# Eight per-partition multiplies, or sixteen, become one broadcast product: the second pass of a decode-attention backward kernel

## The chip, the cores and the metric

The kernel runs on one core of a Trainium2 chip. The metric is device time in microseconds (us), the median of several executions; lower is better. "The kernel before" and "the changed kernel" are the two whose difference is studied.

Names in the views: PE is the matrix engine and PEld its loading of weights; VectorE (DVE), ACT and POOL are the other compute engines; SP only issues transfers here. PSUM holds PE's results (`d_ps` and the other `_ps` tiles in the views). "arena" is one large on-chip buffer from which the kernel cuts its tiles. A transfer is issued on an engine's queue; "lands" means its end in the trace. A store is compute-gated when it has to wait for a result.

## The reference

The reference is the forward pass and all gradients of one decode step: pre-norm attention of one token over the last 4096 positions of a 32768-position cache, then a gated bilinear feed-forward block.

```python
W = 4096; Hq, Hkv, Sk, Dh, D, F = 16, 8, 32768, 256, 448, 1792
k = repeat(k_cache[:, :, Sk - W:, :], 2); v = repeat(v_cache[:, :, Sk - W:, :], 2)
p = softmax(q @ k.T * Dh ** -0.5); o = p @ v
h  = x + o.reshape(1, 1, Hq * Dh) @ wo              # q from layernorm(x) @ wq
h2 = h + ((hn @ w_gate) * (hn @ w_up)) @ w_down      # hn = layernorm(h)
_out, _vjp = jax.vjp(_f, A_x, A_k_cache, A_v_cache, A_wq, A_wo, B_w_gate, B_w_up, B_w_down)
return (_out, *_vjp(grad_out))                       # all tensors bf16
```

What matters for the time is the size of two outputs. The gradients of the two caches have the full shape (1, 8, 32768, 256), 134 MB each. Seven eighths of each lie outside the window and are zeros, but must be written all the same.

## The kernel before

Zeros go out on POOL's queue from the start, a block of 2 MB each, and need no compute. A few zero stores are kept for the end of SP's queue:

```python
late_jobs = [(out_2, G - 1, 5, 7, 2 * ZW), (out_3, G - 1, 0, 6, 2 * ZW), (out_3, G - 1, 6, 7, ZW)]
...
def send_fills(n0, n1, halves=False):
    for reg in fills[n0:n1]:
        ...
            ZQ.dma_start(out=reg, in_=zeros)         # ZQ = nc.gpsimd, POOL's queue (L132)

send_fills(0, HALF0)
send_fills(HALF0, HALF1, True)
# ... first pass over the 8 heads, feed-forward block, then: send_fills(HALF1, len(fills))
```

The second pass makes the gradients of K and V in the window, head by head. For each head it builds eight masked right-hand sides, one for each value of `l`, multiplies by them on PE, copies PSUM to the staging buffers on VectorE and ACT, and stores them through SP's queue (`LD`):

```python
RB_ = Rbig[it % 2]
for l in range(8):
    nc.vector.tensor_scalar(out=RB_[:, l, :], in0=R_sb[:], scalar1=tl_f[:, l:l + 1], scalar2=None, op0=ALU.mult)   # L629
stV, stK = V_sb, kv_at(dK_off[it % 2])
for l in range(8):
    for qp in range(2):
        d_ps = ps_d.tile([128, 2, 2, Dh], f32, tag="d")
        for qi in range(2):
            q = 2 * qp + qi
            nc.tensor.matmul(d_ps[:, qi]..., lhsT=rT[32 * q:32 * (q + 1), :], rhs=RB_[32 * q:32 * (q + 1), l, :], ...)   # L636
        ...                                          # copies: ACT L640, L641; VectorE L643, L644
for o_ap, st_ in ((out_3, stV), (out_2, stK)):
    LD.dma_start(out=o_ap[0, g, Sk - W:, :]..., in_=st_)      # L646: 2.1 MB each
for job in plan[it]:
    job()                                            # weight-gradient rows: dwo, dw_down, dwq, ...
...
for o, g, n0, n1, f in late_jobs:                    # L656: the zero stores on SP's queue
    ...
```

The jobs for dwo and dw_down scale one row of 448 elements by 16 or 14 per-partition factors (the helper's line is L532). Their staging buffers are former V buffers, so a job waits until an earlier store has landed (in the kernel before 13.5 us in all ahead of dwo's rows and 7.1 us ahead of dw_down's). A framework schedules the instructions of each engine when the kernel is built.

Of the kernel before, what the change touches and what calls it, by code (L numbers as in the profile page):

```python
# [10 lines left out]
ALU = mybir.AluOpType  # L11
ACT = mybir.ActivationFunctionType

D = 448
# [7 lines left out]
NF = 14  # L22
# [11 lines left out]
def kernel(  # L34
        ctx, tc, A_x, A_k_cache, A_v_cache, A_wq, A_wo, B_x, B_w_gate, B_w_up, B_w_down, grad_out,
           out_0, out_1, out_2, out_3, out_4, out_5, out_6, out_7, out_8):
    nc = tc.nc
# [15 lines left out]
    def ar(off, n):  # L53
        return arena[:, off:off + n]

    def kv_at(off):
        return ar(off, T * Dh).rearrange("p (t d) -> p t d", d=Dh)
# [38 lines left out]
    dh2_bc = const.tile([128, D], bf16)  # L96
# [53 lines left out]
    tl_f = const.tile([128, 8], f32)  # L150
# [88 lines left out]
    def fill_vpad(i, src):  # L239

        nc.vector.tensor_copy(out=vpad[i][:].rearrange("p e (c w) -> p e c w", w=18)[:, :, :, 0:2],
                              in_=src.unsqueeze(2).to_broadcast([128, 2, 8, 2]))

    def dots(X_sb, XT_slots, pad, rows, cols_pool, cols_tag, evac):

        rows_ps = ps_s.tile([16, 512], f32, tag="rows")
        for q in range(8):
            XT = XT_slots[q % 3]
            tr_ps = ps_tr.tile([128, 2, 4, 128], bf16, tag="tr")
            for dh in range(2):  # L250
                for i in range(4):
                    nc.tensor.transpose(tr_ps[:, dh, i, :], X_sb[:, 4 * q + i, dh * 128:(dh + 1) * 128], ident_bf[:])  # L252
            evac(q, XT, tr_ps[:])
            for dh in range(2):
                nc.tensor.matmul(rows_ps[:], lhsT=pad[:, dh, 16 * q:16 * q + 16], rhs=XT[:, dh].rearrange("p t k -> p (t k)"),  # L255
                                 start=(q == 0 and dh == 0), stop=(q == 7 and dh == 1))
        nc.vector.tensor_copy(out=rows, in_=rows_ps[:])  # L257
        cols_ps = cols_pool.tile([128, 4, 8, 2], f32, tag=cols_tag, name="cols_ps")
        for i in range(4):
            nc.tensor.transpose(cols_ps[:, i].rearrange("p c h -> p (c h)"), rows[:, i * 128:(i + 1) * 128], ident_f[0:16, 0:16])  # L260
        return cols_ps
# [94 lines left out]
    with tc.tile_pool(name="ps_mid", bufs=3, space=bass.MemoryType.PSUM) as ps_mid, \  # L356
# [11 lines left out]
        oX_f = const.tile([128, 32], f32)  # L368
# [17 lines left out]
        hh_f = const.tile([128, NF], f32)  # L386
# [4 lines left out]
        for n in range(len(BLOCKS)):  # L391
# [3 lines left out]
            for b in range(nb):  # L395
                nc.vector.tensor_tensor_reduce(out=dgb[:, 0:D], in0=wd[:, b, :], in1=dh2_bc[:], scale=1.0, scalar=0.0,
                                               op0=ALU.mult, op1=ALU.add, accum_out=d_hh[:, b0 + b:b0 + b + 1])
# [11 lines left out]
            for i in range(2):  # L409
                nc.vector.tensor_tensor(out=diag[:, 0:w].rearrange("p (m b) -> p m b", b=nb), in0=ident_f[:].unsqueeze(2).to_broadcast([128, 128, nb]),  # L410
                                        in1=dgu_f[:, i, cs].unsqueeze(1).to_broadcast([128, 128, nb]), op=ALU.mult)
# [6 lines left out]
            for c in range(4):  # L418
# [3 lines left out]
                                               op0=ALU.mult, op1=ALU.add, accum_out=dhn[0:kp, c, n:n + 1])  # L422
# [9 lines left out]
        dh_bc = const.tile([128, D], bf16)  # L432
# [18 lines left out]
        for jc in range(32):  # L451
            nc.vector.tensor_tensor_reduce(out=wo_sb[:, jc, :], in0=wo_sb[:, jc, :], in1=dh_bc[:], scale=1.0, scalar=0.0,  # L452
                                           op0=ALU.mult, op1=ALU.add, accum_out=doX_f[:, jc:jc + 1])
# [3 lines left out]
                                in1=m8_f[:].unsqueeze(2).to_broadcast([128, 8, 32]), op=ALU.mult)  # L457
# [13 lines left out]
        for dh in range(2):  # L471
# [11 lines left out]
                                scalar1=SCALE, scalar2=None, op0=ALU.mult)  # L483
# [4 lines left out]
    with tc.tile_pool(name="work2", bufs=2) as work2, tc.tile_pool(name="lnw", bufs=1) as lnw, \  # L488
# [17 lines left out]
        for c in range(3):  # L506
            nc.vector.tensor_tensor_reduce(out=wq2A[:, c, :], in0=wq2A[:, c, :], in1=dq_bc, scale=1.0, scalar=0.0,  # L507
                                           op0=ALU.mult, op1=ALU.add, accum_out=dn1[:, c:c + 1])
        for h in range(2):
            nc.vector.tensor_tensor_reduce(out=wq2A[:, 0, 0:HJ], in0=wq2B, in1=dq_bc[:, h * HJ:(h + 1) * HJ], scale=1.0, scalar=0.0,  # L510
                                           op0=ALU.mult, op1=ALU.add, accum_out=dn1[:, 3 + h:4 + h])
# [15 lines left out]
        def buffer():  # L527
            wst_ctr[0] += 1
            return wst[(wst_ctr[0] - 1) % 2]

        def scale_into(out, src, col):
            nc.vector.tensor_scalar(out=out, in0=src, scalar1=col, scalar2=None, op0=ALU.mult)  # L532

        def job_o(n):
            def run():
                buf = buffer()
                for j in range(16):
                    scale_into(buf[:, j * D:(j + 1) * D], dh_bc[:], oX_f[:, 16 * n + j:16 * n + j + 1])
                LD.dma_start(out=out_5.rearrange("(p j) n -> p (j n)", j=32)[:, 16 * n * D:16 * (n + 1) * D], in_=buf[:, 0:16 * D])
            return run  # L540

        def job_d():
            buf = buffer()
            for j in range(NF):
                scale_into(buf[:, j * D:(j + 1) * D], dh2_bc[:], hh_f[:, j:j + 1])
            for f0, nb in BLOCKS:
                b0 = f0 // 128
                LD.dma_start(out=out_8[f0:f0 + 128 * nb, :].rearrange("(p b) n -> p (b n)", b=nb), in_=buf[:, b0 * D:(b0 + nb) * D])
# [38 lines left out]
        def job_qB():  # L587
# [4 lines left out]
            LD.dma_start(out=out_4[384:D, :].rearrange("r (h j) -> (r h) j", h=2), in_=buf[:, 2 * HJ:3 * HJ])  # L592

        plan = [[], [], [job_o(0)], [job_o(1)], [job_d, job_q], [expand_dg, job_qB, job_g(0)], [job_g(1)], []]

        order = [2, 3, 4, 5, 6, 7, 0, 1]
        V2_off = [V_off[g] for g in order[:6]] + [MB, MB + 16 * KB]
        for it, g in enumerate(order):
            V_sb = kv_at(V2_off[it])
            fill_vpad(it % 2, doT_bf[:, :, 2 * g:2 * g + 2])  # L600

            def evac(q, XT, ps):
                if q % 2:
                    nc.scalar.copy(out=XT, in_=ps)  # L604
                else:
                    nc.vector.tensor_copy(out=XT, in_=ps)  # L606
            dpT_ps = dots(V_sb, VT_slot, vpad[it % 2], rows2, ps_t, "tmp", evac)

            pds = work2.tile([128, 4, 8, 4], bf16, tag="pds")
            pv = pT_all[:, g].rearrange("p (q l) h -> p q l h", q=4)  # L610
            tmp = work2.tile([128, T, 2], f32, tag="tmp2")
            nc.vector.tensor_tensor(out=tmp[:], in0=dpT_ps[:].rearrange("p q l h -> p (q l) h"),
                                    in1=delta_bc[:, 2 * g:2 * g + 2].unsqueeze(1).to_broadcast([128, T, 2]), op=ALU.subtract)
            nc.vector.tensor_copy(out=pds[:, :, :, 0:2], in_=pv)
            nc.vector.tensor_tensor(out=pds[:, :, :, 2:4], in0=tmp[:].rearrange("p (q l) h -> p q l h", q=4), in1=pv, op=ALU.mult)
            r_ps = ps_t.tile([128, 128], bf16, tag="tmp")
            nc.tensor.transpose(r_ps[:], pds[:].rearrange("p q l i -> p (q l i)"), ident_bf[:])
            rT = work2.tile([128, 128], bf16, tag="rT")
            nc.vector.tensor_copy(out=rT[:], in_=r_ps[:])
            nc.vector.tensor_copy(out=Zr, in_=Z4[:, :, :, g, :].rearrange("p w e i -> p (w e) i").unsqueeze(2).to_broadcast([128, 4, 32, 4]))  # L620
            R_ps = ps_t.tile([128, 2, 2, 128], f32, tag="tmp")
            for w in range(2):
                for dh in range(2):
                    nc.tensor.matmul(R_ps[:, w, dh, :], lhsT=Zr[:, 2 * w + dh].rearrange("p k i -> p (k i)"), rhs=ident_bf[:], start=True, stop=True)
            R_sb = work2.tile([128, 512], bf16, tag="R", bufs=1)
            nc.scalar.copy(out=R_sb[:], in_=R_ps[:].rearrange("p w e n -> p (w e n)"))
            RB_ = Rbig[it % 2]
            for l in range(8):
                nc.vector.tensor_scalar(out=RB_[:, l, :], in0=R_sb[:], scalar1=tl_f[:, l:l + 1], scalar2=None, op0=ALU.mult)  # L629
            stV, stK = V_sb, kv_at(dK_off[it % 2])  # L630
            for l in range(8):
                for qp in range(2):
# [3 lines that stand above are left out]
                        nc.tensor.matmul(d_ps[:, qi].rearrange("p w d -> p (w d)"), lhsT=rT[32 * q:32 * (q + 1), :], rhs=RB_[32 * q:32 * (q + 1), l, :],  # L636
                                         start=True, stop=True)
                    t = 4 * l + 2 * qp
                    if qp:
                        nc.scalar.copy(out=stV[:, t:t + 2, :], in_=d_ps[:, :, 0, :])  # L640
                        nc.scalar.copy(out=stK[:, t:t + 2, :], in_=d_ps[:, :, 1, :])  # L641
                    else:
                        nc.vector.tensor_copy(out=stV[:, t:t + 2, :], in_=d_ps[:, :, 0, :])  # L643
                        nc.vector.tensor_copy(out=stK[:, t:t + 2, :], in_=d_ps[:, :, 1, :])  # L644
            for o_ap, st_ in ((out_3, stV), (out_2, stK)):
                LD.dma_start(out=o_ap[0, g, Sk - W:, :].rearrange("(p t) d -> p t d", t=T), in_=st_)  # L646
            for job in plan[it]:
                job()
            if it == 6:

                nc.vector.memset(ar(ZW, ZW), 0.0)
# [34 lines left out]
```

## Time and profile before

| | kernel before |
|---|---|
| time, median | 800.08 us |
| bytes moved | 334.80 MB, 216.01 MB of them POOL's zero fills |
| transfer engines | busy in all slices, 419 GB/s on average |
| VectorE (DVE) | 408.4 us busy, 51% |

From the profile's page of the kernel before: busy time of each engine, then the transfers in 40 equal slices of the span (tenths of busy share of the 16 transfer engines, then GB/s), then the totals.

```profile
PE 469.3 (59%) x3159; PEld 242.1 (30%) x3182; DVE 408.4 (51%) x728; ACT 196.2 (25%) x309; POOL 61.4 (8%) x112
...
DMA  9999999999999999999999999999999999999996
GB/s 351 429 432 429 430 430 429 429 429 427 429 422 425 426 419 417 413 423 424 422 423 408 430 429 429 432 424 428 423 429 420 426 424 427 419 424 426 427 436 261
DMA packets 29354, 334.80 MB, mean 419 GB/s; under 512 B 2819, under 2 KB 5894, under 8 KB 7814
```

No compute engine is near full, and the digit of the transfers is 9 everywhere but in the last slice. That could still hide gaps of a few us in the part that the change touches. So here is the busy time in 20 us stretches of the second pass of the kernel before. After each engine's busy us and count come the granted clock of PE, the transfer engines' share (it reads up to 1.03 here) and their GB/s.

```profile
core 0: us, PE busy (x) PEld busy (x) DVE busy (x) ACT busy (x) POOL busy (x), PEclk, DMA share, GB/s
480.00:500.00 20.00, 17.50 (x155) 8.51 (x155) 17.46 (x39) 14.33 (x22) 2.13 (x4) 1.00 1.01 428
...
620.00:640.00 20.00, 0.29 (x1) 0.13 (x2) 3.55 (x2) 0.00 (x0) 1.06 (x2) 0.50 1.02 430
...
720.00:740.00 20.00, 2.54 (x16) 0.52 (x16) 5.60 (x9) 4.84 (x10) 0.00 (x0) 0.50 1.03 426
...
760.00:780.00 20.00, 0.00 (x0) 0.00 (x0) 0.00 (x0) 0.00 (x0) 0.00 (x0) 0.50 1.02 436
780.00:798.40 18.40, 0.00 (x0) 0.00 (x0) 0.00 (x0) 0.00 (x0) 0.00 (x0) 0.50 0.57 246
```

From 620 to 640 us compute all but stopped, waiting for stores to land (one of VectorE's waits for a landing, 23.9 us long, ends at 635.8 us), and the transfer engines didn't notice: share 1.02, 430 GB/s. They had fills to send, issued at 622.5 and 631.8 us.

The timelines of POOL and of SP's queue in the kernel before show how long that lasts. Columns: start, duration, engine, line, operation, count.

```profile
688.23 0.54 POOL L132 DMA_DIRECT2D out_dram<-arena  x1 [16.88 <-issue]
...
727.89 6.93 SPq L646 DMA_DIRECT2D out_dram<-arena  x2
736.57 8.42 SPq L656 DMA_DIRECT2D out_dram<-arena  x3
```

The last fill is issued at 688 us, the last two stores that wait for compute at 728 and 731 us, then zeros. From there to 798 us the queue drains. Bytes issued less bytes landed, summed from the trace's issues and packets, came to 13.6 MB at 730 us. The three zero stores behind the last gated store are not in that sum.

The instructions that the change touches, kernel before, by line and shape: count, busy us, mean ns of one, then idle time of the engine before them. L304 is a tensor product of the first pass that multiplies bf16 by a float32 operand broadcast, as the new products do, so it is a price for the new form: 2284 ns for 2048 columns.

```profile
L304 DVE TENSOR_TENSOR arena<-arena,p_f 128x2048 bf16<-128x2048 bf16 x64 | 145.2, 2284 | 58.7 <-PE M_ps L309 58.7
L629 DVE TENSOR_SCALAR arena<-R_sb,tl_f 128x512 bf16<-128x512 bf16 x64 | 17.8, 347 | 2.1 <-ACT R_sb L626 1.9
L532 DVE TENSOR_SCALAR arena<-dh_bc,oX_f 128x448 bf16<-128x448 bf16 x32 | 8.8, 328 | 13.5 <-DMA out_dram<-arena 13.5
L532 DVE TENSOR_SCALAR arena<-dh_bc,hh_f 128x448 bf16<-128x448 bf16 x14 | 3.9, 329 | 7.1 <-DMA out_dram<-arena 7.1
```

Eight of the L629 multiplies overlap in time: one takes 347 ns, so eight would take 2.78 us end to end, and they fill 2.19. From the timeline of VectorE (columns as in the timelines above), the eight of the first head:

```profile
477.36 2.19 DVE L629 TENSOR_SCALAR arena<-R_sb,tl_f 128x512 bf16<-128x512 bf16 x8 [0.33 <-ACT R_sb L626]
```

### The profile page before, as it was taken

What the parts mean: (1) busy time and instruction counts of PE and PEld (TensorE: products, weight loads), DVE (VectorE), ACT (ScalarE), POOL (GpSimd) and SP (SyncE); (2) the same over time, 40 slices, a digit from 0 to 9 for tenths busy, and PEclk for the clock granted to TensorE, in tenths of its full rate; (3) what the DMA queues carried; (4) which work ended last, traced back from release to release, by engine and by line L of the source; (5) the groups of instructions that cost most, each with busy time, mean ns of one, the idle gap of its engine ahead of it and who ended that gap; (6) DMA issues with size and microseconds to landing.
All of it is one profiled execution on the core that took longest, in us unless ns stands there. A gap on an engine that the chain in (4) does not pass through costs nothing.

```text
span 798.4 us, 7905 instructions
## 1 busy us (share of the span) xinstructions
PE 469.3 (59%) x3159; PEld 242.1 (30%) x3182; DVE 408.4 (51%) x728; ACT 196.2 (25%) x309; POOL 61.4 (8%) x112
## 2 busy tenths in 40 slices
PE   0459999999999998532319568565236027261000
PEld 0334545545445444311207434332103012020000
DVE  2116584765846783143791579467574139573000
ACT  0142314124132201000101127463333016242000
POOL 4000000010101111100210001000000000000000
PEclk9989999999999999555557869785558558565555
DMA  9999999999999999999999999999999999999996
GB/s 351 429 432 429 430 430 429 429 429 427 429 422 425 426 419 417 413 423 424 422 423 408 430 429 429 432 424 428 423 429 420 426 424 427 419 424 426 427 436 261
DMA packets 29354, 334.80 MB, mean 419 GB/s; under 512 B 2819, under 2 KB 5894, under 8 KB 7814
## 3 DMA queue, kind: packets, MB, share of 16 engines
q0 software_dynamic: 16496, 216.01, 64.0%
q1 hardware_dynamic: 11382, 116.68, 34.8%
q10 hardware_dynamic: 1440, 1.61, 0.6%
q8 instruction: 25, 0.41, 0.2%
q14 instruction: 11, 0.09, 0.0%
HBM read 53.69 MB, written 280.59 MB: 419 GB/s over the span
## 4 chain that ended last, share of the span: by engine, by line
PE 40%; DMA 28%; DVE 15%; ACT 4%; issue 2%; another core or an unknown queue 0%; SPq 0%; ACTq 0%; DVEq 0%
DMA out_dram<-arena 18%; PE M_ps L309 13%; PE ok_ps L313 8%; PE rows_ps L255 7%; PE tr_ps L252 5%; DMA dh_bc<-in_grad_out_dram 4%; ACT arena L269 3%; DVE arena L643 2%; DVE arena L644 2%; DMA arena<-in_A_wo_dram 2%; DVE arena L452 2%; PE dqb_ps L495 2%; DMA arena<-in_B_w_up_dram 2%; DMA arena<-in_B_w_gate_dram 2%; DVE arena L421 2%
## 5 line engine op out<-in xcount | busy, mean ns | idle before, releaser
L304 DVE TENSOR_TENSOR arena<-arena,p_f 128x2048 bf16<-128x2048 bf16 x64 | 145.2, 2284 | 58.7 <-PE M_ps L309 58.7
L309 PE MATMUL M_ps<-arena 128*128 128x512 bf16 x489 | 126.4, 381 | 1.1
L255 PE MATMUL rows_ps<-arena,vpad 128*16 128x512 bf16 x256 | 85.6, 430 | 23.1 <-DVE arena L606 17.1
L252 PE MATMUL tr_ps<-ident_bf,arena 128*128 128x128 bf16 x1024 | 87.8, 236 | 14.2 <-DMA arena<-in_A_k_cache_dram 7.2
L132 POOL DMA_DIRECT2D out_dram<-arena x90 | 48.2, 537 | 549.4 <-DMA out_dram<-arena 495.6
L252 PEld LDWEIGHTS <-arena 128*128 128x128 bf16 x1024 | 66.0, 105 | 63.5 <-issue 55.6
L636 PE MATMUL d_ps<-arena,rT 32*128 32x512 bf16 x256 | 44.6, 508 | 67.1 <-DVE arena L644 49.1
L269 ACT COPY arena<-tr_ps 128x1024 bf16<-128x1024 bf16 x64 | 61.7, 1015 | 69.3 <-PE tr_ps L252 69.3
L313 PE MATMUL ok_ps<-arena 128*16 128x256 bf16 x512 | 64.6, 273 | 1.1 <-DVE arena L296 0.9
L309 PEld LDWEIGHTS <-arena 128*128 128x128 bf16 x512 | 43.3, 99 | 51.0 <-issue 15.3
L604 ACT COPY arena<-tr_ps 128x1024 bf16<-128x1024 bf16 x32 | 32.5, 1017 | 95.7 <-PE tr_ps L252 39.1
L640 ACT CAST arena<-d_ps 128x512 bf16<-128x512 f32 x64 | 37.7, 589 | 72.4 <-PE d_ps L636 72.4
L643 DVE CAST arena<-d_ps 128x512 bf16<-128x512 f32 x64 | 43.9, 686 | 14.2 <-PE d_ps L636 14.0
L313 PEld LDWEIGHTS <-arena 128*16 128x16 bf16 x512 | 41.9, 89 | 29.9 <-issue 21.0
L644 DVE CAST arena<-d_ps 128x512 bf16<-128x512 f32 x64 | 43.5, 679 | 7.6 <-DMA out_dram<-arena 7.6
L636 PEld LDWEIGHTS <-rT 32*128 32x128 bf16 x256 | 11.5, 95 | 93.9 <-issue 51.1
L641 ACT CAST arena<-d_ps 128x512 bf16<-128x512 f32 x64 | 38.1, 595 | 7.5 <-DMA out_dram<-arena 7.5
L255 PEld LDWEIGHTS <-vpad 128*16 128x16 bf16 x256 | 19.3, 91 | 57.0 <-issue 49.3
L507 DVE CUSTOM_DVE_ANT_0 arena<-arena 128x4096 bf16<-128x4096 bf16 x3 | 13.1, 4422 | 24.4 <-ACT arena L500 24.4
L284 ACT ACTIVATE e_f<-cols_ps,nbias 128x32 f32<-128x32 f32 x16 | 4.5, 286 | 85.7 <-DVE nbias L280 85.7
L257 DVE COPY arena<-rows_ps 16x512 f32<-16x512 f32 x16 | 10.8, 675 | 28.7 <-PE rows_ps L255 28.7
L606 DVE COPY arena<-tr_ps 128x1024 bf16<-128x1024 bf16 x32 | 21.7, 680 | 3.5 <-PE tr_ps L252 3.4
(198 smaller groups left out, 373.8 us busy)
## 6 DMA issues: line engine op xcount, KB each, us to landing
out_dram<-arena POOLq DMA_DIRECT2D x103, 2048.0 KB, 52.6
out_dram<-arena SPq DMA_DIRECT2D x18, 2048.0 KB, 33.8
arena<-in_A_v_cache_dram SPq DMA_DIRECT2D x10, 2048.0 KB, 49.4
arena<-in_A_k_cache_dram SPq DMA_DIRECT2D x8, 2048.0 KB, 28.6
out_dram<-arena SPq DMA_DIRECT2D x4, 4096.0 KB, 46.1
arena<-in_A_wq_dram SPq DMA_DIRECT2D x2, 3072.0 KB, 20.4
arena<-in_A_wo_dram SPq DMA_DIRECT2D x2, 1792.0 KB, 16.2
out_dram<-arena SPq DMA_DIRECT2D x2, 1792.0 KB, 32.9
```

The costliest lines, as they stand in the source:

```text
L132: ZQ.dma_start(out=reg, in_=zeros)
L252: nc.tensor.transpose(tr_ps[:, dh, i, :], X_sb[:, 4 * q + i, dh * 128:(dh + 1) * 128], ident_bf[:])
L255: nc.tensor.matmul(rows_ps[:], lhsT=pad[:, dh, 16 * q:16 * q + 16], rhs=XT[:, dh].rearrange("p t k -> p (t k)"), start=(q == 0 and dh == 0 ...
L269: sT_ps = dots(kv_at(K_off[g]), KT_slot, vpad[g % 2], rows1, ps_c, "cols", lambda q, XT, ps: nc.scalar.copy(out=XT, in_=ps))
L304: nc.vector.tensor_tensor(out=pK, in0=K_sb[:, 4 * c:4 * c + 4, :].unsqueeze(2).to_broadcast([128, 4, 2, Dh]), in1=p_f[:, c::8, :].unsqueez ...
L309: nc.tensor.matmul(M_ps[:, vh, :], lhsT=V_sb[:, t, vh * 128:(vh + 1) * 128], rhs=pK[:, i, :, :].rearrange("p h d -> p (h d)"), start=(t == ...
L313: nc.tensor.matmul(ok_ps[:, k, :], lhsT=ppad[g % 2][:, 8 * (t % 4) + t // 4, :], rhs=X_sb[:, t, :], start=(g == 0 and k == 0 and t == 0), ...
L636: nc.tensor.matmul(d_ps[:, qi].rearrange("p w d -> p (w d)"), lhsT=rT[32 * q:32 * (q + 1), :], rhs=RB_[32 * q:32 * (q + 1), l, :], start=T ...
L640: nc.scalar.copy(out=stV[:, t:t + 2, :], in_=d_ps[:, :, 0, :])
L641: nc.scalar.copy(out=stK[:, t:t + 2, :], in_=d_ps[:, :, 1, :])
L643: nc.vector.tensor_copy(out=stV[:, t:t + 2, :], in_=d_ps[:, :, 0, :])
L644: nc.vector.tensor_copy(out=stK[:, t:t + 2, :], in_=d_ps[:, :, 1, :])
```

## The change

The intent is fewer VectorE instructions: one broadcast product for a head's eight right-hand sides, one for sixteen rows of dwo, one for fourteen rows of dw_down.

```diff
@@ job_o
-                for j in range(16):
-                    scale_into(buf[:, j * D:(j + 1) * D], dh_bc[:], oX_f[:, 16 * n + j:16 * n + j + 1])
+                nc.vector.tensor_tensor(out=buf[:, 0:16 * D].rearrange("p (j n) -> p j n", n=D), in0=dh_bc[:].unsqueeze(1).to_broadcast([128, 16, D]),
+                                        in1=oX_f[:, 16 * n:16 * n + 16].unsqueeze(2).to_broadcast([128, 16, D]), op=ALU.mult)
@@ job_d
-            for j in range(NF):
-                scale_into(buf[:, j * D:(j + 1) * D], dh2_bc[:], hh_f[:, j:j + 1])
+            nc.vector.tensor_tensor(out=buf[:, 0:NF * D].rearrange("p (j n) -> p j n", n=D), in0=dh2_bc[:].unsqueeze(1).to_broadcast([128, NF, D]),
+                                    in1=hh_f[:].unsqueeze(2).to_broadcast([128, NF, D]), op=ALU.mult)
@@ second pass, each head
-            for l in range(8):
-                nc.vector.tensor_scalar(out=RB_[:, l, :], in0=R_sb[:], scalar1=tl_f[:, l:l + 1], scalar2=None, op0=ALU.mult)
+            nc.vector.tensor_tensor(out=RB_, in0=R_sb[:].unsqueeze(1).to_broadcast([128, 8, 512]),
+                                    in1=tl_f[:].unsqueeze(2).to_broadcast([128, 8, 512]), op=ALU.mult)
```

In each product the factor is broadcast along the innermost axis: one element is read 512 or 448 times in a row (step 0).

## The prediction

> **What bounds it now.** The transfers. The page gives 334.80 MB at a mean of 419 GB/s over 798.4 us, and DMA digit 9 in every slice but the last. The busy time by stretches shows DMA share 1.00 to 1.03 in every 20 us stretch from 480 to 780 us (419 to 436 GB/s), while VectorE is busy 51% of the span. In the second pass two queues feed the same 16 engines: zero fills from POOL, which need no compute, and gradient stores from SP, which do. When SP has nothing to send, the fills take the whole rate (they issue every 5 us instead of every 9). A late store costs nothing while something else is queued. The timeline has the last fill issued at 688 us, the last compute-gated store at 731 us, and three zero stores behind it. Bytes issued minus bytes landed at 730 us: an estimate from the trace's issues and packets is 13.6 MB, some 32 us at 425 GB/s. That is the slack.
>
> **What the change does.** The groups by shape: the multiply by a per-partition scalar takes 347 ns for 512 bf16 columns, 328 ns for 448, but eight in a row fill 2.19 us and sixteen about 3.9 us (0.27 and 0.245 us each, overlapped). A product of two tensors with the float32 one broadcast takes 2284 ns for 2048 columns and 818 for 640: about 1.04 ns a column plus 0.15 us. [...] The new operand is float32, so:
> - masked right-hand sides: 4096 columns, about 4.4 us instead of 2.2, eight times: +18 us
> - dwo: 7168 columns, about 7.6 instead of 3.9, twice: +7 us
> - dw_down: 6272 columns, about 6.7 instead of 3.4: +3 us
>
> Removed: 99 small VectorE instructions. VectorE busy rises from 408 to about 435 us; the second pass is slower on VectorE, not faster.
>
> The built order of instructions moves SP's stores: the first dwo store goes ahead of the third head's, the second dwo store behind dw_down's. Followed by hand with half rate for SP, the heads' stores in the middle come some 20 us later, but landing waits then shorten, and the last compute-gated store comes between 10 us earlier and 20 us later than 731 us. That is inside the 32 us.
>
> **How much is critical.** Nearly nothing. Nothing changes before 477 us. I predict 800.5 us, 797.0 to 804.0 in 8 of 10; faster by over 2%: 1%; within 2%: 96%; slower: 3%.
>
> **What the profile would show.** VectorE busy about 435 us; the new products at 4.4, 7.6 and 6.7 us; DMA digits still 9, 334.8 MB, mean 417 to 421 GB/s; the queue drained by a last store issued near 740 us. Wrong if: products near 2.2 us [...], DMA share under 0.95 in any stretch between 480 and 780 us, or the fills ending early with SP's queue empty.
>
> **What would make it wrong.** A landing wait in the new order that stalls VectorE for over 30 us after the fills have ended leaves the engines idle, and every microsecond of that counts. Or the changed mix of the two queues moves the rate by 1%.

The fit of 1.04 ns a column plus 0.15 us is from the trace, and 18, 7 and 3 us make the 28 us that take VectorE from 408 to about 435 us. "Half rate for SP" is an estimate, from the spacing of the fills in the kernel before: 4.9 us from 388 to 418 us, where SP issues nothing between 385 and 417 us, and 9.3 to 10.1 us from 552 to 610 us, with its stores queued.

## The result, and the profile after

The changed kernel took 799.8 us (median of 4 runs, 799.6 to 799.98); the kernel before took 800.03 in the same rounds. The ratio is 0.9997 with a 95% interval of 0.998 to 1.0015: the same. Ratios here are the mean time of one kernel's fast runs over that of the other's of the same rounds, so not quite the ratio of the medians.

The page of the changed kernel, the same lines as before:

```profile
PE 480.3 (60%) x3159; PEld 245.3 (31%) x3182; DVE 437.0 (55%) x629; ACT 195.9 (25%) x309; POOL 61.4 (8%) x112
...
DMA  9999999999999999999999999999999999999995
GB/s 349 431 431 427 429 431 428 430 429 428 431 425 422 429 420 416 411 423 424 425 426 411 425 432 427 428 426 427 425 425 425 424 423 424 430 420 417 430 437 256
DMA packets 29354, 334.80 MB, mean 419 GB/s; under 512 B 2819, under 2 KB 5894, under 8 KB 7814
```

VectorE has 99 instructions fewer and is busy 28.6 us longer. The transfers are as they were. The new products in the changed kernel, by line:

```profile
L628 DVE TENSOR_TENSOR arena<-R_sb,tl_f 128x4096 bf16<-128x4096 bf16 x8 | 35.4, 4419 | 0.7 <-ACT R_sb L626 0.7
...
L537 DVE TENSOR_TENSOR arena<-dh_bc,oX_f 128x7168 bf16<-128x7168 bf16 x2 | 15.2, 7618 | 0.7 <-ACT arena L641 0.7
...
L544 DVE TENSOR_TENSOR arena<-dh_bc,hh_f 128x6272 bf16<-128x6272 bf16 x1 | 6.7, 6691 | 5.3 <-DMA out_dram<-arena 5.3
```

The eight multiplies of a head filled 2.19 us; the one product takes 4.42 us. The second pass of the changed kernel in stretches, columns as before:

```profile
600.00:620.00 20.00, 0.92 (x14) 0.72 (x12) 4.34 (x5) 1.01 (x1) 1.56 (x3) 0.57 1.01 424
...
720.00:740.00 20.00, 4.29 (x28) 0.76 (x28) 9.71 (x15) 8.10 (x15) 0.00 (x0) 0.50 1.01 416
...
760.00:780.00 20.00, 0.00 (x0) 0.00 (x0) 0.00 (x0) 0.00 (x0) 0.00 (x0) 0.50 1.03 440
780.00:798.20 18.20, 0.00 (x0) 0.00 (x0) 0.00 (x0) 0.00 (x0) 0.00 (x0) 0.50 0.55 236
```

The stretch in which compute stops has moved, and again the transfers go on at full share; no 20 us stretch from 480 to 780 us is below 1.00. The drain has an uneven end: from 792 to 797 us the share is 0.06, as much as one of 16 engines working alone. Which engine that was, the trace does not name, and what an even end would be worth was not tried. The timelines of POOL and SP's queue in the changed kernel:

```profile
675.32 0.54 POOL L132 DMA_DIRECT2D out_dram<-arena  x1 [11.52 <-issue]
...
735.98 1.13 SPq L646 DMA_DIRECT2D out_dram<-arena  x1
740.01 4.82 SPq L656 DMA_DIRECT2D out_dram<-arena  x3
```

The last compute-gated store is issued at 736.0 instead of 731.3 us, and the last fill 13 us earlier, at 675 instead of 688: while SP's stores were late, fills took their place. PE's waits moved. These are its waits on the right-hand sides and on two steps before them, kernel before and then changed kernel (us in total, times, longest us):

```profile
PE d_ps L636 <- DVE arena L629: 4.5, 4, 1.2
PE r_ps L617 <- DVE pds L615: 26.2, 3, 23.8
PE R_ps L624 <- DVE rT L619: 23.9, 5, 12.6
```

```profile
PE d_ps L636 <- DVE arena L628: 33.1, 5, 21.8
PE r_ps L617 <- DVE pds L615: 0.7, 1, 0.7
PE R_ps L624 <- DVE rT L619: 0.5, 1, 0.5
```

The wait on the products is 28.6 us longer, but one wait of 21.8 us is not the length of a 4.4 us product, and the two earlier waits are 48.9 us shorter. So these lines alone don't show that PE lost time. VectorE's own waits for stores to land did shrink, kernel before and then changed kernel:

```profile
DVE arena L532 <- DMA out_dram<-arena: 42.0, 5, 11.5
DVE arena L651 <- DMA out_dram<-arena: 23.9, 1, 23.9
DVE arena L644 <- DMA out_dram<-arena: 7.6, 1, 7.6
```

```profile
DVE arena L532 <- DMA out_dram<-arena: 22.0, 2, 15.4
DVE arena L651 <- DMA out_dram<-arena: 11.9, 1, 11.9
DVE arena L644 <- DMA out_dram<-arena: 10.6, 2, 6.0
DVE arena L544 <- DMA out_dram<-arena: 5.3, 1, 5.3
DVE arena L553 <- DMA out_dram<-arena: 2.4, 1, 2.4
```

That is 73.5 us before and 52.2 after: of the 28.6 us of added VectorE work, about 21 are matched by shorter waits for landings, and the last gated store is only 4.7 us later. The bytes still queued then had only these 4.7 us to hide. How much of the shorter waits is due to the changed order of SP's stores, no run separates. The time did not move.

### The profile page after: what moved, and what is told of

Its sections match the earlier page's. It is cut to its first block, busy times and chain, and to the rows that moved or that the text cites. A ratio compares the mean times of both kernels' runs of the same rounds, so it can differ in the third digit from the quotient of the medians.

```text
span 798.2 us, 7807 instructions
## 1 busy us (share of the span) xinstructions
PE 480.3 (60%) x3159; PEld 245.3 (31%) x3182; DVE 437.0 (55%) x629; ACT 195.9 (25%) x309; POOL 61.4 (8%) x112
## 4 chain that ended last, share of the span: by engine, by line
DMA 47%; another core or an unknown queue 15%; DVE 14%; PE 9%; issue 3%; ACT 2%; POOL 1%; SPq 0%; DVEq 0%; ACTq 0%; POOLq 0%
DMA out_dram<-arena 47%; DVE arena L628 2%; DVE arena L452 2%; PE dqb_ps L495 2%; DVE arena L643 2%; PE rows_ps L255 2%; PE d_ps L636 2%; PE tr_ps L252 1%; DVE arena L644 1%; DVE arena L507 1%; POOL out_dram L132 1%; DVE arena L421 1%; PE dqb_ps L498 1%; DVE arena L537 1%
## 5 line engine op out<-in xcount | busy, mean ns | idle before, releaser
L304 DVE TENSOR_TENSOR arena<-arena,p_f 128x2048 bf16<-128x2048 bf16 x64 | 145.2, 2284 | 58.7 <-PE M_ps L309 58.6
L636 PE MATMUL d_ps<-arena,rT 32*128 32x512 bf16 x256 | 46.9, 531 | 111.0 <-DVE arena L644 63.8
L252 PE MATMUL tr_ps<-ident_bf,arena 128*128 128x128 bf16 x1024 | 91.7, 241 | 18.8 <-ACT arena L604 11.3
L255 PE MATMUL rows_ps<-arena,vpad 128*16 128x512 bf16 x256 | 90.4, 451 | 20.6 <-DVE arena L606 14.6
L252 PEld LDWEIGHTS <-arena 128*128 128x128 bf16 x1024 | 68.4, 108 | 70.7 <-issue 62.7
L309 PEld LDWEIGHTS <-arena 128*128 128x128 bf16 x512 | 43.3, 99 | 50.9 <-issue 15.2
L628 DVE TENSOR_TENSOR arena<-R_sb,tl_f 128x4096 bf16<-128x4096 bf16 x8 | 35.4, 4419 | 0.7 <-ACT R_sb L626 0.7
## 6 DMA issues: line engine op xcount, KB each, us to landing
out_dram<-arena SPq DMA_DIRECT2D x2, 1792.0 KB, 15.6
```

What stands on the lines that cost most here:

```text
L252: nc.tensor.transpose(tr_ps[:, dh, i, :], X_sb[:, 4 * q + i, dh * 128:(dh + 1) * 128], ident_bf[:])
L255: nc.tensor.matmul(rows_ps[:], lhsT=pad[:, dh, 16 * q:16 * q + 16], rhs=XT[:, dh].rearrange("p t k -> p (t k)"), start=(q == 0 and dh == 0 ...
L304: nc.vector.tensor_tensor(out=pK, in0=K_sb[:, 4 * c:4 * c + 4, :].unsqueeze(2).to_broadcast([128, 4, 2, Dh]), in1=p_f[:, c::8, :].unsqueez ...
L309: nc.tensor.matmul(M_ps[:, vh, :], lhsT=V_sb[:, t, vh * 128:(vh + 1) * 128], rhs=pK[:, i, :, :].rearrange("p h d -> p (h d)"), start=(t == ...
L628: nc.vector.tensor_tensor(out=RB_, in0=R_sb[:].unsqueeze(1).to_broadcast([128, 8, 512]), in1=tl_f[:].unsqueeze(2).to_broadcast([128, 8, 51 ...
L636: nc.tensor.matmul(d_ps[:, qi].rearrange("p w d -> p (w d)"), lhsT=rT[32 * q:32 * (q + 1), :], rhs=RB_[32 * q:32 * (q + 1), l, :], start=T ...
```

## The experiments

Theory A: bytes over rate set the time; the change adds some 28 us of VectorE work, and the transfers (waits for landings before the last gated store, bytes still queued after it) hide it. Rival B: VectorE's own idle time takes the longer products up, fills or no fills. Rival C: the chain of waits that ends last, through landings and VectorE, sets the time, and the change happens to leave its length as it was.

### Without the fills, before and after

```diff
-    send_fills(0, HALF0)
-    send_fills(HALF0, HALF1, True)
+    # no zero fills from POOL
...
-                send_fills(HALF1, len(fills))
+                pass
```

Two of the nine outputs are wrong (parts are never written). All runs without fills show times, not results. The runs below were taken in three sets on different chips; the kernel before took 800.22, 800.19 and 799.93 us in them.

> The kernel before without POOL's zero fills (216 of 334.8 MB): wrong output on purpose unless the outputs start as zeros. Both theories expect it far under 800 us, since the traffic shrinks to 119 MB; I estimate 640 to 710 us: the first pass is held by PE and stays, the second pass loses about half of its 145 us of landing waits. This is the base for the run beside it.

> The changed kernel without POOL's fills. Theory A (the change costs VectorE time, and it is the queued fills that hide it): slower than the kernel before without fills by 8 to 28 us (1.2 to 4.3%), the added VectorE work being 28 us. Rival B (VectorE's own idle time, half of the second pass, takes the longer products up, fills or no fills): within 3 us of it.

Measured: 643.15 us (642.2 to 644.5) without the change and 668.22 us (667.9 to 668.6) with it. The change costs 25.1 us, 3.9%, once the fills are gone. The second pass in one window of 204 us, first the kernel before without fills, then the changed kernel without fills; columns as in the other stretches:

```profile
426.00:630.00 204.00, 122.01 (x890) 53.83 (x888) 155.85 (x339) 102.58 (x168) 0.00 (x0) 0.74 0.71 297
```

```profile
426.00:630.00 204.00, 126.06 (x889) 55.62 (x887) 183.76 (x240) 102.58 (x168) 0.00 (x0) 0.73 0.59 245
```

The transfer share is now 0.71 and 0.59, and VectorE rises from 155.9 to 183.8 us of 204. Of 27.9 us added in this window, 25 show in the time. PE's waits for VectorE's copies out of PSUM grow by 21.7 us, kernel before and then changed kernel, both without fills:

```profile
PE d_ps L636 <- DVE arena L644: 19.2, 24, 1.5
```

```profile
PE d_ps L636 <- DVE arena L644: 40.9, 31, 5.8
```

Rival B, "fills or no fills", falls: here VectorE's idle time doesn't absorb the work. In these two runs VectorE waits for no store to land in the second pass. A weaker form of B stays: with the fills, most of the added work is matched by time in which VectorE no longer waits for landings.

### Fewer bytes

```diff
-                send_fills(HALF1, len(fills))
+                send_fills(HALF1, len(fills) - 4)
```

> The changed kernel with 4 of its zero fills left out (8.39 MB; wrong output on purpose unless the outputs start as zeros). Theory A (bytes over rate set the time): 8.39 MB at 425 GB/s less, 19.7 us, so about 780 us. Rival C (the chain of waits that ends last, through the landings and VectorE, sets the time): it holds no fill, and the time stays at 800 us or falls by less than 5 us.

Measured: 780.45 us, 19.8 us below the 800.22 of the kernel before in the same rounds (ratio 0.9755). 8.39 MB at 425 GB/s are 19.7 us. Only the four fills were taken out; the built order of SP's stores is the same as in the changed kernel. The last gated store is issued at 732.8 us instead of 736.0, so the compute chain became some 3 us shorter and the time 19.8. Rival C falls.

### How much delay is free

The last head's product is computed more than once, which leaves the results right:

```diff
-            nc.vector.tensor_tensor(out=RB_, in0=R_sb[:]...
+            for _ in range(17 if it == 7 else 1): nc.vector.tensor_tensor(out=RB_, in0=R_sb[:]...
```

with 17, 9 and 25 in the three kernels. The scheduler reacts: it puts the three remaining zero stores (10.5 MB) ahead of the last head's stores, so more is queued in front of these than in the changed kernel.

> The changed kernel with the last head's product of right-hand sides computed 17 times instead of once: 16 x 4.3 to 4.4 us = 70 us more of VectorE just before the last two gated stores; results stay right. The build puts the three remaining zero stores ahead of these stores. The last stores were issued at 735.7 us; 70 us later they are issued at 806, and 4.19 MB then need about 10 to 12 us. Theory A (slack is what is queued): about 818 us, that is +18 to +20 us, not +70. Rival C (VectorE is on the chain that sets the time): about 870 us.

> The changed kernel, fills kept, with the last head's product computed 9 times: about 35 us more of VectorE before the last gated stores, which are then issued at about 770 us and need 11 us, as in the run with 16 repeats: 781, before the 797 us at which the queue runs empty anyway. Theory A: 799 to 801 us, no change at all. Rival C: 835 us.

> The same with 24 repeats. With 16 the engines stood idle from about 790 to 803 us and the time was 815.2. Past that point every microsecond counts: 8 more repeats of 4.3 us give 34.5 us more, 848 to 852 us.

| repeats added | VectorE work added | measured | last gated store issued |
|---|---|---|---|
| 0 | 0 | 799.8 us | 736 us |
| 8 | 35.5 us | 799.92 us (799.7 to 800.1) | 765 us |
| 16 | 71 us | 815.2 us (812.8 to 817.5) | 804 us |
| 24 | 106.5 us | 851.54 us (848.6 to 853.0) | 839 us |

Each repeat takes 4.44 us in the traces. The first 8 repeats are free: ratio 1.0, interval 0.9985 to 1.0015. From 8 to 16 the work grows by 35.5 us and the time by 15.3; from 16 to 24 the time grows by 36.3. That is the picture of a queue: delay costs nothing until the queue is empty, then all of it. An estimate for this order: of the 71 us of 16 repeats some 56 were free (71 less the 15.4 by which the time is above 799.8). Once it is empty, 4.2 MB take some 11 us: in the run with 16 repeats the last stores are issued at 803.4 and 804.0 us and land by 814.6.

The stretches of the run with 24 repeats show the empty queue, columns as before:

```profile
760.00:780.00 20.00, 0.00 (x0) 0.00 (x0) 19.83 (x6) 0.00 (x0) 0.00 (x0) 0.50 0.97 419
780.00:800.00 20.00, 0.00 (x0) 0.00 (x0) 19.86 (x5) 0.00 (x0) 0.00 (x0) 0.50 0.09 37
800.00:820.00 20.00, 0.00 (x0) 0.00 (x0) 19.83 (x6) 0.00 (x0) 0.00 (x0) 0.50 0.00 0
```

The transfer share falls from 0.97 to 0.09 and 0: here the prediction's warning sign appears, and here the time goes up.

One line of the run with 8 repeats is worth keeping. It is the chain of waits from 705 us to the end, by line (shares of that window):

```profile
by line: DVE arena L628 42.5%; PE d_ps L636 6.9%; DVE arena L643 6.4%; DVE arena L644 5.2%; issue 1.2%; ACT R_sb L626 0.7%; DVEq L681 0.6%; ACT arena L640 0.5%
```

The chain puts 42.5% of the window down to the repeated product, though taking all eight repeats out again changes nothing. The chain is followed back from the last instruction, and the last instruction is not what ends last here: the last gated store is issued at 765 us, and the queue drains until 797.

### Which part costs what, without the fills

Two kernels without fills, each with one half of the change: the right-hand sides alone (the last hunk of the diff), and the rows of dwo and dw_down alone (the first two).

> Without POOL's fills, the change to the masked right-hand sides alone. The whole change cost 25 us there (668.2 beside 643.2). Theory A1 (each head waits for its right-hand sides): 8 x 2.2 = 18 us more than the kernel before without fills, 656 to 664 us. Rival A2 (the long row products, 7.6 us in front of evictions, cost the most): under 10 us more, below 653. Wrong output in the two large gradients on purpose, as in the run it is compared with.

> Without POOL's fills, the change to the dwo and dw_down rows alone. A1: 4 to 10 us more than the kernel before without fills, 647 to 653 us, the two parts adding up to about 25 us. A2: 15 us more or over.

Measured, against 643.15 us: the right-hand sides alone 660.42, that is +17.3; the rows alone 657.66, that is +14.5. The first fits A1 and the second fits neither, being just under the 15 of A2. The parts sum to 31.8 us, more than the 25.1 of the whole. VectorE's busy time on the page of these runs rises by 18.7 us (426.1 less 407.4) and by 10.4 us (417.8 less 407.4). So the rows cost more than their own work. The order of SP's stores differs between these builds, so the split between the two parts is not clean; that each build costs over 14 us without the fills is shown.

### Why the product takes 4.4 us

In the prediction I put the slow rate down to the float32 operand. Two variants test that. The first makes the mask operand bf16 and keeps the broadcast, fills kept. The second, without fills, lays a bf16 mask of 8 x 64 columns out in memory and broadcasts it along a middle axis, so the innermost step is 1 everywhere:

```diff
+tl_b = const.tile([128, 8], bf16); nc.vector.tensor_copy(out=tl_b[:], in_=tl_f[:])
-                                    in1=tl_f[:].unsqueeze(2).to_broadcast([128, 8, 512]), op=ALU.mult)
+                                    in1=tl_b[:].unsqueeze(2).to_broadcast([128, 8, 512]), op=ALU.mult)
```

```diff
+mask = ar(RB + 49 * KB, KB).rearrange("p (l n) -> p l n", l=8)
+nc.vector.tensor_copy(out=mask, in_=tl_f[:].unsqueeze(2).to_broadcast([128, 8, 64]))
...
+nc.vector.tensor_tensor(out=RB_.rearrange("p l (r n) -> p l r n", n=64), in0=R_sb[:].rearrange("p (r n) -> p r n", n=64).unsqueeze(1).to_broadcast([128, 8, 8, 64]),
+                        in1=mask.unsqueeze(2).to_broadcast([128, 8, 8, 64]), op=ALU.mult)
```

> The changed kernel (fills kept) with the mask operand of the right-hand sides' product made bf16, still broadcast along the innermost axis with step 0. Theory F [...]: about 2.28 us a product. Rival S (the step of 0 holds it there whatever the type): 4.42 us. The total stays within 1 us of 800 either way.

> Without POOL's fills, the changed kernel with a bf16 mask of 8 x 64 columns laid out in memory, so that all three tensors of the right-hand sides' product are bf16 and step by one element. [...] the product takes about 2.28 us (half of 4.27, plus 0.15) instead of 4.42, and the time comes back to that of the run with the rows' change alone, within 3 us. [...] 4.4 us and 668 us.

Theory F is that the float32 operand holds the product at its 4.42 us. The second text has two branches: if the dense form is faster, 2.28 us; if not, 4.4 us and 668 us.

The products by line, first of the bf16 mask with step 0, then of the dense bf16 mask:

```profile
L628 DVE TENSOR_TENSOR arena<-R_sb,tl_b 128x4096 bf16<-128x4096 bf16 x8 | 35.3, 4418 | 0.7 <-ACT R_sb L626 0.7
```

```profile
L630 DVE TENSOR_TENSOR arena<-R_sb,arena 128x4096 bf16<-128x4096 bf16 x8 | 18.3, 2284 | 0.7 <-ACT R_sb L628 0.6
```

The type alone changes nothing: 4418 ns beside 4419. With bf16 and an innermost step of 1 the product takes 2284 ns. So the step of 0 is enough to hold the product at 4.4 us, and rival S is right. L304, with float32 and a step of 0, took the same 2284 ns for half the columns, 2048. Whether float32 with an innermost step of 1 would be held back too, no run here shows.

The total of the first variant was 800.24 us (a single run, state unknown), no different from 800.19. The total of the second was 664.4 us (662.2 to 665.2), not within 3 us of the 657.66 of the run with the rows' change alone: 6.7 us remain although one dense product takes as long as the eight scalar multiplies did.

### One product or eight, at the same rate

```diff
+for l in range(8):
+    nc.vector.tensor_tensor(out=RB_[:, l, :].rearrange("p (r n) -> p r n", n=64), in0=R_sb[:].rearrange("p (r n) -> p r n", n=64), in1=mask[:, l:l + 1, :].to_broadcast([128, 8, 64]), op=ALU.mult)
```

> Without POOL's fills. The dense bf16 mask run came out 6.7 us slower than the run with eight scalar multiplies (664.4 beside 657.7) though its product takes 2.28 us, as long as the eight did. Here the dense product is cut into eight products of 512 columns, the order of SP's stores the same as with one. Theory G (one long product makes the first matmuls of a head wait for all eight parts): back to 657 to 660 us, although VectorE works about 0.5 to 1 us longer a head. Rival O (the order of instructions, which moved with the change, costs the 6.7 us): 664 us or more.

Measured: 661.19 us (660.0 to 661.3), outside both expectations. Cutting the product up takes back 3.2 of the 6.7 us, although VectorE works longer on it (22.4 us busy in total instead of 18.3). Why is not shown. Theory G had the first matmuls of a head wait for the long product, but in the traces PE waits 3.0 us in all for the one product and 6.3 us for the eight. What shrinks is its wait for VectorE's copies, one product and then eight:

```profile
PE d_ps L638 <- DVE arena L646: 40.8, 33, 6.2
```

```profile
PE d_ps L638 <- DVE arena L646: 33.1, 26, 5.8
```

A long product that stands in front of copies would give this, but no run tests it. The other half of the 6.7 us stays open too; the order of SP's stores in these two builds differs from that of the rows-only build and may account for it, but no run shows that.

## Why the prediction was right

- "The transfers" bound the kernel, and nearly nothing of the change is critical: right. Taking 8.39 MB away took 19.8 us away; adding 35.5 us of VectorE work took nothing.
- VectorE "busy rises from 408 to about 435 us": 437.0. The products "at 4.4, 7.6 and 6.7 us": 4.42, 7.62, 6.69. The durations came from other instructions of the trace before, mainly L304, whose factor has the same innermost step of 0; that is why they held although the reason was incomplete.
- The reason given for the rate, "the new operand is float32, so", was incomplete. With a bf16 operand it stays at 4.42 us, because of the innermost step of 0; bf16 with a step of 1 took 2.28 us. The sizes did not depend on that reason; someone who had acted on it and only changed the type would have gained nothing.
- "The heads' stores in the middle come some 20 us later": too small. The fourth head's were issued at 611 instead of 575 us and the fifth's at 646 instead of 601. "But landing waits then shorten": the first dwo store landed after 15.6 us instead of 32.9. By the sixth head the lag is 7 us. So the lag in the middle was mis-sized by about a factor of two, and the shorter waits made up for it.
- The last gated store "between 10 us earlier and 20 us later than 731 us": 4.7 us later. "Inside the 32 us" of slack: yes. The slack itself wasn't measured in the predicted order of stores, because the scheduler reordered the zero stores in the delayed kernels. There at least 35.5 us of added work were free.
- DMA share under 0.95 would have shown it wrong: it stayed at 1.00 or more in every 20 us stretch from 480 to 780 us. The fills did end early, by 13 us, but SP's queue was not empty then: the share from 660 to 700 us is 1.01.
- What the result alone could not have shown is that the change does cost something: 25.1 us as soon as the transfers are no longer the limit. "Same" here means hidden.

Of what was tried, only taking bytes away shortened the time. With the fills in place, neither the changed form of these products nor its bf16 variant did; the dense form was not run there. None of the runs with all outputs right beat the kernel before clear of the noise.

## What to carry to other kernels

Where the transfer engines are at full share from end to end and work that needs no compute is queued, ask how many us of bytes still stand in the queue when the last compute-gated store is issued: that is about the delay that is free there, and the chain of waits doesn't show it. Here that was an estimate of 32 us from 13.6 MB; in the delayed kernels, with 10.5 MB more in front, an estimate of some 56 us. Earlier in the kernel, look for waits for landings, which can take added work up too (73.5 us of them before, 52.2 after). Fewer instructions are not less work: eight fast multiplies overlapped in 2.19 us and one broadcast product took 4.42, so price the form from the trace, and look at the innermost step as well as the type (both bf16, 4096 columns: 4418 ns with a step of 0, 2284 with a step of 1). With the same operation and step, grouping did save busy time: 18.3 us for eight dense products, 22.4 for the same cut into 64. To learn whether a change that moved nothing is harmless or only hidden, take the limit away (here the fills) from both kernels and time them again.
